# SyncE's transfers limited to five under way, a warm-up of two long matmuls, and inputs of 48 rows in an FFT convolution with two gated MLPs

## The chip, the cores and the metric

The kernel runs on one core of a Trainium2 chip. The metric is the device time of one execution in microseconds; the time before is 1123.38 us, the median of three runs (1122.09 to 1124.87). A profile of one execution comes with it. TensorE, VectorE, ScalarE and GpSimd compute, and SyncE issues the transfers on one queue in program order; 16 DMA engines carry them, and the engines' own code too.

## The reference, cut to what matters

```python
X = np.fft.rfft(x, axis=1)                      # x: (2, 3008, 256)
y = np.fft.irfft(X * (filt_r + 1j * filt_i), n=3008, axis=1)
x = y.reshape(6016, 256)
g = x @ w_gate                                  # first MLP, d_ff 1536
x = (g / (1 + exp(-g)) * (x @ w_val)) @ w_out
h = x @ w_in                                    # second MLP, d_ff 2048
out = (h * clip(h + 3, 0, 6) / 6) @ w_out2
```

## The kernel before, in words

The 3008-point transform is split into 47 x 64 points. Its inputs lie in DRAM as 128 rows: rows 0 to 46 hold one half of a column group, rows 64 to 110 the other half, and the rows between are zeros. The matmuls of L332 read only rows 0 to 47 and 64 to 111 (`rows(r, N1P)`, `N1P = 48`).

The transform works in 16 steps of one column group each (`STEPS`, loop `for k in range(N + 2)` at L463). A step k runs `over_n1(k)` (L332: 32 small matmuls, each two passes of 48 columns), then `back(k - 2)` (L374: 8 matmuls of two passes), then a list of transfers (`moves[k]`), then `over_n2(k)` (L348: 8 matmuls of two passes) and `filter_product(k)` (VectorE L361, GpSimd L115 and L118). ScalarE copies between the stages (L339, L340, L379). The list of a step holds `load_x(k + 3)` (steps 1 to 12), two transfers of a filter (`load_filter`, steps 2 to 5), the weights of the first MLP in three parts (`load_dec`, steps 1, 8, 11), and stores of finished quarters to the DRAM tile `d2` (`store`, two in each of the steps 5 to 12, eight in step 13). At step 12 the first halves of two token blocks are loaded back from `d2` (`load_half`, L441), 48 rows at a time, and at step 15 the second halves, which need the eight stores of step 13.

`load_x(k)` fills one of four places in a ring: it waits until `over_n1(k - 4)` has read the place. The first input goes on ScalarE's queue, every other on SyncE's, each in two transfers: by column quarters for k < 2, by column halves of all 128 rows after that. How many transfers are under way is not set by the kernel; the tile framework gives each one of a small set of semaphores in turn.

Ahead of the first input TensorE runs `idle(8)` (L317), eight matmuls of 128 columns on zeros, with a memset before them (L311).

After the transform come the first MLP on the first block (L233, L241), in which the other stores of `d2` and the weights of the first MLP still move, and then both MLPs on all blocks (L680, L725), untouched by the change except that the writes of decoded weights (`low_w1`, L404) and `load_dec` now go through the new helper.

Of the kernel before, what the change touches and what calls it, by code (L numbers as in the profile page):

```python
# [16 lines left out]
P = 128  # L17
B, S, D = 2, 3008, 256
N1, N2 = 47, 64
N1P = 48  # L20
# [57 lines left out]
def fft_conv_glu_mlp(ctx: ExitStack, tc: tile.TileContext, x, filt, mats, sgn, w1, w2, out):  # L78
    nc = tc.nc
    w1, w2 = w1.bitcast(U32), w2.bitcast(U32)  # L80
# [9 lines left out]
    sg = keep.tile([P, NK], F32, name="sg")  # L90
# [7 lines left out]
    def wall(f):  # L98
        return wall_a[:, f] if f < 8 else wall_b[:, f - 8]


    d2 = [dram.tile([NK, P, D], F32, name=f"d2_{b}") for b in range(B)]
    yd = [dram.tile([P, 4, 512], F32, name=f"yd_{k}") for k in range(len(BLOCKS))]
    w1f = [dram.tile([P, 10 * P], F32, name=f"w1f_{f}") for f in range(F1)]
# [5 lines left out]
    def bank(tag="gv"):  # L110
        turn[tag] += 1
        return banks[tag][(turn[tag] - 1) % 4]

    def minus(out, a, b, engine=None):
        (engine or nc.vector).tensor_tensor(out=out, in0=a, in1=b, op=ALU.subtract)  # L115
# [9 lines left out]
    def rows(i, n=64):  # L125

        return slice(i * 64, i * 64 + n)
# [4 lines left out]
    def turns(first, n):  # L132

        return 32 * first // N1, -(-(32 * first + n // 2) // N1)
# [132 lines left out]
    with tc.manual_schedule():  # L267
# [7 lines left out]
        fl = [a[:, :3072].rearrange("p (j r n) -> p j r n", j=4, r=2) for a in (x0, side)]  # L275
        ring = work.tile([P, 7168], F32, tag="xs", name="ring")
        turned = work.tile([P, 7168], F32, tag="xs", name="turned")[:, :6144].rearrange("p (b q c) -> p b q c", b=2, c=P)
        room = new_y()

        N, RING = 16, 2  # L280
        STEPS = [(b, 4 * a + i) for a in range(2) for b in range(B) for i in range(4)]
        xin, first, spec, acc2 = {}, {}, {}, {}

        def load_x(k, engine=nc.sync):
            b, j = STEPS[k]
            if k % 2 == 0:
                xin[k // 2] = ring[:, k // 2 % RING * 2048:(k // 2 % RING + 1) * 2048].rearrange("p (a n) -> p a n", a=2)
            to, src = (v.rearrange("p (o i n) -> p i o n", o=2, i=2) if k < 2 else v.rearrange("p (i n) -> p i n", i=2)
                       for v in (xin[k // 2][:, k % 2], x[b, j // 2, :, j % 2]))
            for i in range(2):  # L290
                engine.dma_start(out=to[:, i], in_=src[:, i])

        def load_filter(j):
            for r in range(2):
                nc.sync.dma_start(out=fl[j // 4][:, j % 4, r], in_=filt[j][:, r])

        load_x(0, nc.scalar)
        load_x(1)
        nc.sync.dma_start(out=sg, in_=sgn)
        load_filter(0)  # L300
        load_filter(1)
        load_x(2)
        load_filter(2)
        load_x(3)
        load_filter(3)
# [1 line left out]
        nc.gpsimd.memset(warm, 0.0)  # L307
        nc.scalar.activation(out=warm, in_=warm, func=AF.Silu)

        blank = turned[:, 1, 0]  # L310
        nc.vector.memset(blank, 0.0)  # L311

        def idle(n):

            acc = bank()
            for _ in range(n):
                nc.tensor.matmul(acc[:, :P], blank, blank)  # L317

        idle(8)

        def prepare_filter(j):

# [57 lines left out]

        def store(b, a, i):
            q = slice(i * NK // 8, (i + 1) * NK // 8)
            nc.sync.dma_start(out=d2[b][q, :, a * P:(a + 1) * P].rearrange("q p c -> p q c"), in_=turned[:, b, q])  # L383

        def words(a):
            return a.bitcast(U32).rearrange("p (n t) -> p n t", t=2)
# [3 lines left out]
        def load_dec(f, n=1):  # L390
            a = x0[:, (f + 1) % 2 * 3072:]
            dec[f] = Decode(None, None, 768, (words(a[:, :1536]), a[:, 1536:2304], a[:, 2304:3072]))
            raw = dec[f].raw.rearrange("p n t -> p (n t)")
            for i in range(n):
                c = slice(1536 * i // n, 1536 * (i + 1) // n)
                nc.sync.dma_start(out=raw[:, c], in_=w1[:, f, c])

        def high_w1(f):
            nc.scalar.copy(out=wall(f)[:, 0], in_=dec[f].w)
# [1 line left out]
        def low_w1(f, engine=None):  # L401
            w = dec.pop(f).w
            minus(wall(f)[:, 1], w, wall(f)[:, 0].bitcast(F32), engine)
            nc.sync.dma_start(out=w1f[f][:, :6 * P], in_=w)  # L404

        todo = {}

# [9 lines left out]
        for k, f in ((1, 0), (8, 1), (11, 2)):  # L417
            send(k, load_dec, f, 3)
        for j in range(4, 8):
            send(j - 2, load_filter, j)  # L420
        for i in range(8):
            send((5, 5, 6, 6, 7, 7, 8, 8)[i], store, 0, 0, i)
            send((9, 9, 10, 10, 11, 11, 12, 12)[i], store, 1, 0, i)
            send(13, store, 0, 1, i)

        for f, steps in ((0, (4, 5, 5, 6, 7, 8, 9, 10, 10)), (1, (10, 11, 11, 12, 12, 13, 14, 15, 17)), (2, (15, 15, 15, 17))):
            at(steps[0], lambda f: dec[f].start(), f)
            for i in range(len(steps[1:7])):
                at(steps[1 + i], lambda f, i: dec[f].part(i, nc.vector), f, i)
            if f < 2:  # L430
                at(steps[7], high_w1, f)
                at(steps[8], low_w1, f)
            else:
                for i in range(3, 6):
                    at(N + 1, lambda f, i: dec[f].part(i, nc.vector), f, i)

        def load_half(j, a, g):
            t0, t1 = turns(FIRST[j][0], 512)
            g = g[:, :7 * P].rearrange("p (t c) -> p t c", c=P)
            for r in range(2):  # L440
                nc.sync.dma_start(out=g[rows(r, N1P), :t1 - t0],  # L441
                                  in_=d2[0].rearrange("q (h n) c -> (q h) n c", h=2)[:, 32 * r + t0:32 * r + t1, a * P:(a + 1) * P])
            return g

        half_accs = {}
# [17 lines left out]
        for k in range(N + 2):  # L463
            if 1 < k < N:
                over_n1(k)
            if 2 <= k <= N:
                back(k - 2)
            for step, *a in moves.get(k, ()):
                step(*a)
            if k == 12:  # L470
                g0 = new_g()
                gt[0] = [load_half(0, 0, g0)]
                gt[1] = [load_half(1, 0, room[:, 6 * COLS:])]
            elif k == N - 1:
                gt[0].append(load_half(0, 1, g0[:, 7 * P:]))
                gt[1].append(load_half(1, 1, turned[:, 0].rearrange("p q c -> p (q c)")))
            if k < N:
                over_n2(k)
                filter_product(k)
            elif k == N:  # L480
                for j in range(2):
                    form(j, 0)
                    form_end(j, 0)
            if k < 3 or 3 < k < 8:
                prepare_filter(k + (k < 3))
            for step in todo.get(k, ()) if k <= N else ():
                step()
# [80 lines left out]
        for t in range(2 * plain):  # L568
            p, i = divmod(t, 2)
            k, g_ = steps[p]  # L570
            f = 2 * g_ + i
# [8 lines left out]
            if t == 0:  # L580
                pairs = []
                for u in range(2):
                    if u:
                        back(N - 1)
                        turn["gv"] -= 2
                        for step in todo[N + 1][:3]:
                            step()
                        load_dec(3)
                        form(0, 1)
                        form_end(0, 1)  # L590
                        for step in todo[N + 1][3:]:
                            step()
                    pairs.append((bank(), bank()))
                    gate, val = pairs[u]
                    for part in ((0, 1, 2),) if u else ((0, 2), (1,)):
                        l1(gate, wall(u), (3 * P, 4 * P), xsd[k], part, depth=(0,))
                        l1(val, wall(u), (0, 5 * P), xsd[k], part, depth=(0,))
# [13 lines left out]
            h = hid[p][:, i]  # L611
            nc.scalar.activation(out=h, in_=gate, func=AF.Silu)

            lead, rest, part = ([f_ for f_ in range(2, F1) if t == 2 * f_ + d + (f_ > 9)] for d in (-6, -5, -4))
# [7 lines left out]
            for f_ in part:  # L622
                low_w1(f_, nc.gpsimd)
                if f_ + 2 < F1:
                    load_dec(f_ + 2)
# [16 lines left out]
            if 10 < t < 23:  # L642
                q, r = divmod(t - 11, 2)
# [86 lines left out]
        class Plain:  # L730
            kind, k, f, n, last = 0, 0, 0, 512, True
# [125 lines left out]
        for s in range(S):  # L857
# [15 lines left out]
            k, f, n, kind = u.k, u.f, u.n, u.kind  # L873
# [121 lines left out]
```

## Time and profile before

| What | Value |
|---|---|
| median of three runs | 1123.38 us |
| the profiled execution | 1120.58 us, span 1118.8 |
| TensorE, matmuls | 1108.6 us, 99% of the span |
| VectorE | 858.3 us, 77% |
| ScalarE | 751.9 us, 67% |
| GpSimd | 602.3 us, 54% |
| chain of waits, TensorE's share | 94% |
| HBM read, written | 117.27 MB, 32.24 MB |

The transform takes about the first 58 to 75 us of the span, two of the page's 40 slices. A row of the chain of waits gives the start, the length and who holds the chain; "issue" is time in which an engine waits for nothing that the profile shows. Rows of SyncE (SPq) give the time that issuing takes, not the transfer. The end of a matmul is modelled, so a group's end is later than the start of what follows it.

### The profile page before, as it was taken

The page shows a single profiled execution, that of the slowest core. Times are in us where ns is not written, and L with a number is a line of the kernel's source. Part 1 is how long each engine was busy: PE and PEld are TensorE (multiplying, and loading weights), DVE is VectorE, ACT ScalarE, POOL GpSimd, SP SyncE. Part 2 cuts the span into 40 slices and gives each one's busy share as a digit, 9 for nine tenths or more (in the row PEclk, how much of TensorE's full clock was granted, in tenths as well). Part 3 has the DMA queues.
Part 4 walks back from the last instruction along what each step waited for, and adds up shares of the span by engine and source line. Part 5 has one row for each costly group of instructions (what it writes and reads, how often), then busy time and mean ns, then how long its engine had stood idle before and what let it go on. Part 6 is the DMA issues. An engine that isn't in the chain of part 4 may idle for free.

```text
span 1118.8 us, 19197 instructions
## 1 busy us (share of the span) xinstructions
PE 1108.6 (99%) x7246; PEld 924.9 (83%) x7246; DVE 858.3 (77%) x1168; ACT 751.9 (67%) x1367; POOL 602.3 (54%) x779
## 2 busy tenths in 40 slices
PE   9999999999999999999999999999999999999998
PEld 7678887888888888888899888888888888888997
DVE  5889976778878788786888868667677677677765
ACT  4554447667767667766777777777777677677764
POOL 4652375795765576484587645335435444354440
PEclk9999999999999999999999999999999999999999
DMA  9974954844633552263353421422322412412300
GB/s 315 296 210 132 278 186 157 223 152 134 200 118 111 147 176 100 83 202 104 102 208 120 162 82 60 153 78 71 135 78 78 144 62 78 149 52 77 117 27 33
DMA packets 58844, 150.75 MB, mean 135 GB/s; under 512 B 5568, under 2 KB 26016, under 8 KB 56992
## 3 DMA queue, kind: packets, MB, share of 16 engines
q1 hardware_dynamic: 58208, 149.01, 41.4%
q8 instruction: 56, 0.92, 0.3%
q10 hardware_dynamic: 544, 0.52, 0.2%
q14 instruction: 36, 0.29, 0.1%
HBM read 117.27 MB, written 32.24 MB: 134 GB/s over the span
## 4 chain that ended last, share of the span: by engine, by line
PE 94%; DVE 3%; DMA 1%; ACT 1%; issue 1%; SPq 0%; ACTq 0%; DVEq 0%
PE gv L680 44%; PE a L725 36%; PE gv L233 5%; PE a L241 2%; PE gv L374 2%; PE a L348 1%; PE gv L332 1%; PE gv L157 1%; DVE hs L115 1%; DVE h L707 1%; DVE xs L115 1%; DMA ring<-x_in 0%; DVE raw L115 0%; SPq L383 0%; DMA d<-turned 0%
## 5 line engine op out<-in xcount | busy, mean ns | idle before, releaser
L680 PE MATMUL gv<-xs,wu 128*128 128x512 f32 (+1 forms) x2268 | 567.1, 386 | 0.1
L115 POOL TENSOR_TENSOR wu<-st,wu 128x224 fp32r<-128x224 f32 x432 | 311.9, 753 | 397.0 <-ACT wu L517 397.0
L680 PEld LDWEIGHTS gv<-xs,wu 128*128 128x128 f32 x2268 | 423.7, 188 | 81.3 <-ACT raw L546 1.7
L725 PE MATMUL a<-hs,wo 128*128 128x512 f32 (+1 forms) x1872 | 476.7, 385 | 0.0
L725 PEld LDWEIGHTS a<-hs,wo 128*128 128x128 f32 x1872 | 351.4, 188 | 65.4 <-ACT hs L713 0.3
L115 DVE TENSOR_TENSOR hs<-h,hs 128x512 fp32r<-128x512 f32 (+3 forms) x228 | 235.4, 1033 | 66.8 <-ACT hs L713 62.3
L713 ACT CAST hs<-h 128x512 fp32r<-128x512 f32 (+3 forms) x216 | 172.6, 799 | 128.8 <-DVE h L709 73.9
L115 POOL TENSOR_TENSOR wo<-st,wo 128x256 fp32r<-128x256 f32 x156 | 148.8, 967 | 0.0
L709 DVE SCALAR_TENSOR_TENSOR h<-h,gv 128x512 f32<-128x512 f32 (+1 forms) x144 | 96.5, 670 | 22.7 <-ACT h L703 22.4
L517 ACT CAST wu<-st 128x384 fp32r<-128x384 f32 x216 | 110.6, 563 | 0.3 <-DMA st<-w1f 0.3
L701 ACT ACTIVATE h<-gv 128x512 f32<-128x512 f32 (+1 forms) x120 | 70.7, 589 | 58.3 <-PE gv L680 57.2
L118 DVE TENSOR_TENSOR gv<-gv,h 128x512 f32<-128x512 f32 (+1 forms) x108 | 74.0, 685 | 41.4 <-PE gv L680 35.7
L703 ACT ACTIVATE h<-gv 128x512 f32<-128x512 f32 (+1 forms) x144 | 84.1, 584 | 15.3 <-PE gv L680 15.1
L890 ACT COPY gv<-gv 128x512 f32<-128x512 f32 (+1 forms) x108 | 60.9, 564 | 42.6 <-PE gv L680 38.4
L118 DVE TENSOR_TENSOR h<-gv,h 128x512 f32<-128x512 f32 (+1 forms) x108 | 72.9, 675 | 18.5 <-PE gv L680 18.1
L709 DVE SCALAR_TENSOR_TENSOR h<-h,h 128x512 f32<-128x512 f32 (+1 forms) x48 | 32.7, 681 | 58.6 <-ACT h L703 58.6
L894 ACT COPY h<-gv 128x512 f32<-128x512 f32 (+1 forms) x108 | 62.5, 579 | 16.4 <-PE gv L680 13.4
L707 DVE TENSOR_TENSOR h<-h 128x512 f32<-128x512 f32 (+1 forms) x60 | 61.4, 1023 | 1.7 <-ACT h L701 1.0
L115 DVE TENSOR_TENSOR xs<-raw,xs 128x512 fp32r<-128x512 f32 (+1 forms) x77 | 58.9, 767 | 0.1
L517 ACT CAST wo<-st 128x256 fp32r<-128x256 f32 (+1 forms) x108 | 54.2, 501 | 0.0
L560 ACT CAST xs<-raw 128x512 fp32r<-128x512 f32 (+1 forms) x77 | 45.7, 609 | 2.9 <-DVE raw L115 2.8
L233 PE MATMUL gv<-xs,wall_a 128*128 128x512 f32 x192 | 45.7, 392 | 0.1
(88 smaller groups left out, 899.7 us busy)
## 6 DMA issues: line engine op xcount, KB each, us to landing
st<-w1f SPq DMA_DIRECT2D x60, 576.0 KB, 3.8
st<-w2f SPq DMA_DIRECT2D x48, 704.0 KB, 4.1
raw<-w_in SPq DMA_DIRECT2D x16, 512.0 KB, 4.6
ring<-x_in SPq DMA_DIRECT2D x30, 256.0 KB, 5.5
x<-w_in SPq DMA_DIRECT2D x9, 768.0 KB, 5.4
d<-turned SPq DMA_DIRECT2D x32, 192.0 KB, 5.3
yd<-y SPq DMA_DIRECT2D x5, 1024.0 KB, 6.5
raw<-yd SPq DMA_DIRECT2D x5, 1024.0 KB, 6.3
```

What stands on the lines that cost most here:

```text
L115: (engine or nc.vector).tensor_tensor(out=out, in0=a, in1=b, op=ALU.subtract)
L118: (engine or nc.vector).tensor_tensor(out=out, in0=a, in1=b, op=ALU.add)
L233: nc.tensor.matmul(acc, w[:, r, c[k]:c[k] + P], xs[:, v, k], start=(r, v, k) == (0, 0, 0), stop=(r, k) == (1, 1), skip_group_check=len(dep ...
L517: nc.scalar.copy(out=to[:, 0, at:at + hi - lo], in_=src[:, lo:hi])
L680: nc.tensor.matmul(acc[:, :n], w[:, r, FORM[a] * P:(FORM[a] + 1) * P], xs_part(k, v, i), start=start and q == 0, stop=q == 2, skip_group_c ...
L701: nc.scalar.activation(out=self.value(t, 0), in_=src, func=AF.Silu)
L703: nc.scalar.activation(out=self.value(t, a), in_=src, func=AF.Relu, bias=3.0)
L707: nc.vector.tensor_tensor(out=self.value(t, 0), in0=self.value(t, 0), in1=src, op=ALU.mult)
L709: nc.vector.scalar_tensor_tensor(out=self.value(t, a), in0=self.value(t, a), scalar=6.0, in1=src, op0=ALU.min, op1=ALU.mult)
L713: nc.scalar.copy(out=self.hs[:, t, :, 0, :self.n], in_=self.value(t))
L725: yield lambda t=t, v=v, a=a, j=j, r=r: nc.tensor.matmul(banks["a"][2 * j + t][:, :n], self.wo[:, r, (2 * a + j) * P:(2 * a + j + 1) * P], ...
L894: nc.scalar.copy(out=u.s7, in_=b3[:, :n])
```

## The change

A helper `move` replaces the direct calls in the transform. It keeps a list of SyncE's transfers and makes each one wait for the landing of the fifth before it. Inputs from the third on are read as two transfers of 48 whole rows (4 KB a row) in place of two of 128 half rows (2 KB a row). The memset and the idle matmuls are four times as wide, and there are two in place of eight.

```diff
-        N, RING = 16, 2
+        N, RING, MOST_UNDER_WAY = 16, 2, 5
+        under_way = []
+
+        def move(to, src, engine=nc.sync):
+
+            ins = engine.dma_start(out=to, in_=src)
+            if engine is nc.sync:
+                if len(under_way) >= MOST_UNDER_WAY:
+                    tc.add_manual_dep(ins.ins, under_way[-MOST_UNDER_WAY].ins.name,
+                                      mybir.DependencyInfo(mybir.DependencyClass.Sync, mybir.DependencyReason.DATA),
+                                      reason="few transfers under way")
+                under_way.append(ins)
...
-            to, src = (v.rearrange("p (o i n) -> p i o n", o=2, i=2) if k < 2 else v.rearrange("p (i n) -> p i n", i=2)
-                       for v in (xin[k // 2][:, k % 2], x[b, j // 2, :, j % 2]))
+            to, src = xin[k // 2][:, k % 2], x[b, j // 2, :, j % 2]
+            if k < 2:
+                to, src = (v.rearrange("p (o i n) -> p i o n", o=2, i=2) for v in (to, src))
             for i in range(2):
-                engine.dma_start(out=to[:, i], in_=src[:, i])
+                part = (slice(None), i) if k < 2 else rows(i, N1P)
+                move(to[part], src[part], engine)
...
-        blank = turned[:, 1, 0]
+        blank = turned[:, 1, 0:4].rearrange("p q c -> p (q c)")
         nc.vector.memset(blank, 0.0)
...
-                nc.tensor.matmul(acc[:, :P], blank, blank)
-
-        idle(8)
+                nc.tensor.matmul(acc, blank[:, :P], blank)
+
+        idle(2)
```

The filters, the sign table, the stores, `load_dec`, the writes of `low_w1` and `load_half` call `move` in the same way; `load_g`, `load_wq` and what follows the transform do not.

## Rows read from the trace of the kernel before

**Rows 1.** Chain of waits, 11 to 56 us: start, length (us), what held it.
```profile
11.54 0.86 issue
...
21.98 1.17 PE a L348 x15
...
25.63 1.17 PE a L348 x15
...
27.67 0.25 issue
...
33.25 0.31 issue
...
43.54 1.06 issue
...
49.95 1.39 issue
...
55.72 1.17 PE a L348 x14
```

**Rows 2.** The page, parts 1 and 3: records of TensorE, packets of its code.
```profile
PE 1108.6 (99%) x7246; PEld 924.9 (83%) x7246; DVE 858.3 (77%) x1168; ACT 751.9 (67%) x1367; POOL 602.3 (54%) x779
...
q8 instruction: 56, 0.92, 0.3%
```

**Rows 3.** Transfers from 42.20 to 43.25 us: all packets, and those of code.
```profile
DMA packets 40, 0.07 MB, mean 69 GB/s; under 512 B 5, under 2 KB 18, under 8 KB 38
...
q8 instruction: 1, 0.02, 5.8%
```

**Rows 4.** Busy us of each engine by stretch, clock, DMA share, GB/s.
```profile
10.00:20.00 10.00, 9.14 (x238) 6.94 (x232) 7.74 (x16) 4.29 (x12) 7.67 (x12) 1.00 1.00 349
...
30.00:40.00 10.00, 9.69 (x270) 7.51 (x266) 9.73 (x16) 4.87 (x14) 7.37 (x10) 1.00 1.03 328
...
58.00:60.00 2.00, 2.00 (x32) 1.40 (x26) 2.00 (x4) 1.85 (x6) 1.56 (x3) 1.00 1.03 268
70.50:72.00 1.50, 1.38 (x87) 1.27 (x79) 1.47 (x3) 1.50 (x5) 1.50 (x3) 1.00 1.16 179
117.50:119.50 2.00, 2.00 (x10) 1.66 (x9) 1.97 (x3) 1.09 (x3) 0.00 (x0) 1.00 1.01 135
```

**Rows 5.** SyncE's issues, 12 to 18 us; from the page, KB and us to landing.
```profile
12.43 1.52 SPq L396 DMA_DIRECT2D x<-w_in  x3
...
17.17 0.85 SPq L291 DMA_DIRECT2D ring<-x_in  x2
...
ring<-x_in SPq DMA_DIRECT2D x30, 256.0 KB, 5.5
```

**Rows 6.** Instructions in order of time, 0 to 13 us: start, us.
```profile
0.83 0.17 DVE L311 MEMSET turned<- 128x128 f32 x1 [0.83 <-PEq L980]
...
4.76 1.11 PE L332 MATMUL gv<-mat,ring 48*64 48x48 f32 x32
...
6.17 1.61 PE L332 MATMUL gv<-mat,ring 48*64 48x48 f32 x96 [0.30 <-DMA ring<-x_in]
...
11.80 0.91 POOL L115 TENSOR_TENSOR h<-h 128x192 f32<-128x192 f32 x1
...
12.76 1.74 PE L374 MATMUL gv<-h,mat 64*64 64x384 f32 x14
```

**Rows 7.** SyncE and TensorE in order of time, 52 to 75 us.
```profile
52.87 0.98 SPq L291 DMA_DIRECT2D ring<-x_in  x2
...
60.29 5.43 SPq L383 DMA_DIRECT2D d<-turned  x8
...
64.19 1.21 PE L332 MATMUL gv<-mat,ring 48*64 48x48 f32 x60
...
68.36 0.82 SPq L441 DMA_DIRECT2D g<-d  x2
...
74.84 0.84 PE L157 MATMUL a<-mat,g 48*64 48x47 f32 x48
```

More of the change, by code (lines that the diff above doesn't have):

```diff
@@ L287, in load_x @@
                 xin[k // 2] = ring[:, k // 2 % RING * 2048:(k // 2 % RING + 1) * 2048].rearrange("p (a n) -> p a n", a=2)
-            to, src = (v.rearrange("p (o i n) -> p i o n", o=2, i=2) if k < 2 else v.rearrange("p (i n) -> p i n", i=2)
-                       for v in (xin[k // 2][:, k % 2], x[b, j // 2, :, j % 2]))
+            to, src = xin[k // 2][:, k % 2], x[b, j // 2, :, j % 2]
+            if k < 2:
+                to, src = (v.rearrange("p (o i n) -> p i o n", o=2, i=2) for v in (to, src))
             for i in range(2):
-                engine.dma_start(out=to[:, i], in_=src[:, i])
+                part = (slice(None), i) if k < 2 else rows(i, N1P)
+                move(to[part], src[part], engine)
         def load_filter(j):
             for r in range(2):
-                nc.sync.dma_start(out=fl[j // 4][:, j % 4, r], in_=filt[j][:, r])
+                move(fl[j // 4][:, j % 4, r], filt[j][:, r])
         load_x(0, nc.scalar)
         load_x(1)
-        nc.sync.dma_start(out=sg, in_=sgn)
+        move(sg, sgn)
         load_filter(0)
@@ L382, in store @@
             q = slice(i * NK // 8, (i + 1) * NK // 8)
-            nc.sync.dma_start(out=d2[b][q, :, a * P:(a + 1) * P].rearrange("q p c -> p q c"), in_=turned[:, b, q])
+            move(d2[b][q, :, a * P:(a + 1) * P].rearrange("q p c -> p q c"), turned[:, b, q])
         def words(a):
@@ L395, in load_dec @@
                 c = slice(1536 * i // n, 1536 * (i + 1) // n)
-                nc.sync.dma_start(out=raw[:, c], in_=w1[:, f, c])
+                move(raw[:, c], w1[:, f, c])
         def high_w1(f):
@@ L403, in low_w1 @@
             minus(wall(f)[:, 1], w, wall(f)[:, 0].bitcast(F32), engine)
-            nc.sync.dma_start(out=w1f[f][:, :6 * P], in_=w)
+            move(w1f[f][:, :6 * P], w)
         todo = {}
@@ L440, in load_half @@
             for r in range(2):
-                nc.sync.dma_start(out=g[rows(r, N1P), :t1 - t0],
-                                  in_=d2[0].rearrange("q (h n) c -> (q h) n c", h=2)[:, 32 * r + t0:32 * r + t1, a * P:(a + 1) * P])
+                move(g[rows(r, N1P), :t1 - t0], d2[0].rearrange("q (h n) c -> (q h) n c", h=2)[:, 32 * r + t0:32 * r + t1, a * P:(a + 1) * P])
             return g
```

## The prediction

> **What bounds the kernel now.** I read the page first: TensorE is busy for 99% of the span and nearly all of the chain of waits is TensorE, so only time in which it stands still can be won. I then took the chain of waits in order of time over the transform, since the change touches nothing later. It is a loop of three kinds of TensorE work per step (L332, L374, L348), and the reader should see two things in it. The L348 pieces of undisturbed steps start 3.65 us apart (21.98, 25.63), and five times the chain stands at "issue", a wait for nothing that the profile shows: 0.86, 0.25, 0.31, 1.06 and 1.39 us, together 3.87 us [rows 1].
>
> These look like waits for TensorE's own code. They stand in the middle of an L332 or an L374 group whose operands are all there. The page counts 7246 + 7246 records on TensorE and 56 packets (0.92 MB, so 16 KB each) in its instruction queue, one per 259 records [rows 2]; a step has 64 + 16 + 16 passes, 192 records, so a block lasts 1.35 steps. For the 1.06 us stop I cut the transfers to a window: the block arrives between 42.20 and 43.25 us, when hardly anything else moves (69 GB/s) [rows 3]; TensorE goes on at 44.61. So the block came late. Why is seen around it: from 10 to 20 and from 30 to 40 us the 16 DMA engines are at a share of 1.00 and 1.03 [rows 4], and SyncE issues far ahead. In four rows, of which the first and the last are shown, it issues nine transfers from 12.43 to 18.02 us, and one takes some 5.5 us to land [rows 5]: about eight are under way, and the block stands among them.
>
> **The change, part by part.** The sum is made against the profiled execution, 1120.58 us (span 1118.8 and 1.8 around it). The median of the runs shown is 1123.38, 2.8 us more; I add the difference to that.
>
> *Stops for code.* From the L348 piece at 21.98 to that at 55.72 lie eight steps [rows 1]: 33.74 us where 8 x 3.65 = 29.20 would do, an excess of 4.54. Four of the stops lie in between (3.01 us); the other 1.5 us is what a stop costs beyond what is shown, because the last passes before it are drawn until they drain and the loop needs a step to settle. With five under way instead of eight, a block that waits as a transfer does would come after 5/8 of 5.5 us, some 3.4 us, and blocks are wanted some 4.9 us apart (1.35 x 3.65). I take all 4.54 us back here; the bounds are 0 and 4.54. Something is lost to VectorE: from 30 to 40 us it is busy for 9.73 of 10 us [rows 4], so a loop that is 12% faster there (4.54 of 38 us) can't all be had in those steps; later ones have room. 0.3 us, from 0 to 0.5.
>
> The first stop (0.86 us at 11.54) gives nothing: the L374 passes behind it start at 12.76, and GpSimd hands over their operand at 11.80 + 0.91 = 12.71 [rows 1, 6].
>
> *Warm-up.* Two matmuls of 512 columns instead of eight of 128: the same 1024 columns. Its memset takes 0.17 us for 128 columns; for 512 it is between 0.17 and 0.68, so the warm-up starts and ends 0 to 0.5 us later [rows 6]. [...] I take 0.
>
> *The cap at the start.* load_x(0) is on ScalarE's queue and does not count. The first wait is that of filter 1, for load_x(1). From there each SyncE instruction waits for the landing five back, and all issues behind it wait with it. The third input is wanted at about 10.2 us, and even at 11.6 it would be in time for the L374 at 12.76, whose operand comes from GpSimd. I take 0, from 0 to +0.5.
>
> *Inputs as 48 rows.* Bytes fall from 2 x 256 KB to 2 x 192 KB per input. What a byte costs is the disputed term. 128-row loads move at 349 GB/s with the engines full (10 to 20 us) [rows 4]. The loads of 48 rows that the kernel already has (g) do not: with the engines as full, 135 GB/s in the long ones and 179 in the short ones at 70.5 us, where nothing was queued ahead; but 268 in 58 to 60 us, where the short ones stood in a deep queue among stores [rows 4]. So a pair that costs 524 KB / 349 = 1.50 us now costs 393 KB / 268 = 1.47 us at best and 393 KB / 135 = 2.9 us at worst. A queue of five is between the two: I take 200 GB/s, 1.97 us, +0.47 us per input. [...]
>
> [...]
>
> *Is that hidden?* The last input is issued at 52.87 and 53.4, lands 5 to 5.5 us later at about 58.7, and is used at 64.19: 5.5 us of slack [rows 5, 7]. If TensorE comes 4.5 us earlier, 1.0 is left. The inputs 5 to 15 are read while the engines are full: 11 x 0.47 = 5.2 us later. So 5.2 - 1.0 = 4.2 us of waiting for inputs takes the place of the stops, at 200 GB/s. Not all of these steps are full (42.2 to 43.25 us is nearly empty), and stores and filters between them keep their price; I take off 0.7 for that one gap: 3.5.
>
> *The end of the transform.* The eight stores at 60.29 are let go by ScalarE, and behind them wait the four loads of the second half (from 68.36 on), first read by L157 at 74.84 [rows 7]. At the 179 GB/s of that window two of 147 KB need 1.65 us; with the 2 us or so that pass before it, some 2 to 3 us of slack stand before 74.84. With five under way the last stores come up to 0.5 us later, which this slack covers while TensorE is only about 1 us ahead; if it were 4 ahead, the stores would be let go earlier too.
>
> Sum: -4.54 + 3.5 = -1.04 us, and with VectorE's 0.3 -0.7; between the two I take -1.0. 1120.58 - 1.0 = 1119.6, and on the median 1122.4.
>
> **Rivals.** *Faster: the halves run side by side.* For it: 268 GB/s at 58 to 60 us in a queue, and the bytes fall by a quarter. Then an input costs 1.47 us, the slack of 1.0 is enough, and all stops go: -4.54 + 0.3 (VectorE) = -4.2, 1119.2 on the median. [...]
>
> *Slower: inputs become the bound.* For it: 135 to 179 GB/s wherever 48-row loads stood alone. At 165 GB/s, between these two, a pair costs 2.38 us, +0.88; 11 x 0.88 - 1.0 = 8.7 us of starving against 4.54 won: +4.2, 1127.6. It decides where the pair costs more than 1.50 + (4.54 + 1.0)/11 = 2.0 us, below 196 GB/s. The last slack of the stores goes with it.
>
> *No change: the cap does not bring the code earlier.* If a block waits for a fixed share of work whatever is queued, the stops stay, inputs stay hidden behind them and the time is 1123.4, within 0.5. For it: at 42.2 us the block came late though little else moved. [...]
>
> **How the numbers follow.** Chances: forecast 0.37, side by side 0.30, inputs the bound 0.18, no change 0.15. The forecast's own range is 1119.5 to 1125 (150 to 230 GB/s in part of the steps). The range over all, with the 1.3 us by which runs differ, is 1118.3 to 1127.3. A measurement tells 0.3%, 3.4 us, from no change: faster means under 1120.0, slower over 1126.8. Side by side lands under 1120.0 in four of five cases (0.24) and the forecast in one of six (0.06): 0.30. Slower: 0.12 of the 0.18 and 0.03 of the forecast: 0.15. Between: 0.55.
>
> **What would show it.** In the chain after: no "issue" pieces over 0.2 us in the L332 and L374 groups (if they stay, the third rival). "DMA ring<-x_in" as what ends L332's idle time, some 3.5 us in all; none if the halves run side by side, over 7 if inputs are the bound. GB/s at a full share between 15 and 50 us: near 200 in the forecast, 270 or more in the first rival. The L348 piece of step 12 starts at 55.72 now [rows 1]; I expect 54 to 55. I am wrong in the main if TensorE waits neither for code nor for inputs and the time still stands, or if something after 75 us moves.

## The result and the profile after

The changed kernel takes 1127.21 us (median of 11 runs, 1125.12 to 1132.41), the kernel before 1121.06 us on the same chip (11 runs): a ratio of 1.0057, 95% interval 1.0042 to 1.0073, 6 us slower. I had forecast 1122.4, 1 us below the 1123.38 known then, too little to tell from no change. The profiled execution took 1126.81 us (span 1125.0); its clock is 1.00 throughout. The lines of the kernel moved: L332 is L346, L348 is L362, L374 is L388, L379 is L393, and every transfer of the transform is issued in L285.

The chain of waits of the changed kernel, the pieces that answer to [rows 1] and the whole end of the transform (start, length, what held it):

```profile
12.65 1.08 PE gv L346 x59
...
20.00 4.63 DMA ring<-x_in
...
29.35 0.38 issue
...
48.78 2.53 DMA ring<-x_in
...
58.49 1.17 PE a L362 x15
...
62.09 3.42 DMA ring<-x_in
...
65.54 4.67 DMA g<-d
...
70.23 3.61 DMA d<-turned
...
73.85 2.76 DMA d<-turned
...
77.06 3.38 DMA g<-d
...
80.48 0.89 PE a L157 x40
```

The stops for code are gone: of 3.87 us of "issue" pieces one of 0.38 is left. In their place stand transfers. The piece at 48.78 is named after the input that was issued then, but that input landed at 52.15. What let ScalarE go on at 51.31 was the last of the early stores of `turned`, issued at 46.77 and landed at 51.21, and TensorE waited for ScalarE (the idle time stands in brackets):

```profile
51.31 0.86 ACT L393 COPY turned<-gv 128x384 f32<-128x384 f32 x2 [4.61 <-DMA ring<-x_in]
51.94 1.80 PE L388 MATMUL gv<-h,mat 64*64 64x384 f32 x16 [2.98 <-ACT turned L393]
```

ScalarE may not overwrite `turned` before its store has landed.

From 62.09 on the chain is nothing but transfers of 2.8 to 4.7 us, each released by the landing of one before it. Up to the store at 73.85 that is the cap, drawn as a chain; the loads behind it need the stores, as they did before. The L348 piece of step 12 (now L362) starts at 58.49 in place of 55.72, and L157's second half at 80.48 in place of 74.84 [rows 7], 5.64 us later. Nothing behind it gives this back or adds much: 1126.81 - 1120.58 is 6.2.

The start, the windows, and SyncE, as in [rows 4 to 7]; then SyncE's longest waits up to 85 us (total, times, longest):

```profile
0.91 0.48 DVE L325 MEMSET turned<- 128x512 f32 x1 [0.91 <-PEq L993]
5.17 2.56 PE L346 MATMUL gv<-mat,ring 48*64 48x48 f32 x128
12.26 0.95 PE L346 MATMUL gv<-mat,ring 48*64 48x48 f32 x25 [1.48 <-DMA ring<-x_in]
```

```profile
10.00:20.00 10.00, 8.43 (x203) 6.38 (x200) 7.31 (x15) 4.22 (x12) 7.30 (x12) 1.00 0.89 221
30.00:40.00 10.00, 10.00 (x230) 7.67 (x224) 9.84 (x17) 6.42 (x18) 7.83 (x11) 1.00 0.86 230
```

```profile
15.85 3.12 SPq L285 DMA_DIRECT2D x<-w_in  x3
...
62.09 1.52 SPq L285 DMA_DIRECT2D ring<-x_in  x2
...
68.51 5.77 SPq L285 DMA_DIRECT2D d<-turned  x8
76.69 0.91 SPq L285 DMA_DIRECT2D g<-d  x2
```

```profile
SPq L285 <- DMA ring<-x_in: 13.5, 22, 1.7
SPq L285 <- DMA d<-turned: 6.1, 10, 1.8
SPq L285 <- DMA x<-filt_in: 4.1, 3, 1.8
```

The engines are no longer full (shares 0.89 and 0.86 where they were 1.00 and 1.03) and yet TensorE waits for data: SyncE stands still until an earlier transfer lands, 24 us in these three rows; before, the longest row of this kind was 3.8 us (inputs). The first load of w_in and the last input are 52 transfers apart in the program, in both kernels. Before, SyncE needed 40.44 us for them (12.43 to 52.87), now 46.24 (15.85 to 62.09). The eight stores of step 13 go out at 68.51 in place of 60.29, the loads of the second half at 76.69 in place of 68.36.

### The profile page after: what moved, and what is told of

Same layout as the page of the kernel before. It is cut to its first block, busy times and chain, and to the rows that moved or that the text cites. A ratio compares the mean times of both kernels' runs of the same rounds, so it can differ in the third digit from the quotient of the medians.

```text
span 1125.0 us, 19173 instructions
## 1 busy us (share of the span) xinstructions
PE 1109.7 (99%) x7234; PEld 921.3 (82%) x7234; DVE 857.2 (76%) x1168; ACT 751.7 (67%) x1367; POOL 603.2 (54%) x779
## 4 chain that ended last, share of the span: by engine, by line
PE 93%; DMA 3%; DVE 3%; ACT 1%; issue 0%; SPq 0%; ACTq 0%; DVEq 0%
PE gv L693 44%; PE a L738 36%; PE gv L233 5%; PE a L241 2%; DMA ring<-x_in 2%; PE gv L157 1%; PE gv L388 1%; PE a L362 1%; PE gv L346 1%; DMA g<-d 1%; DVE hs L115 1%; DVE h L720 1%; DMA d<-turned 1%; DVE xs L115 1%; DVE raw L115 0%
## 5 line engine op out<-in xcount | busy, mean ns | idle before, releaser
L115 POOL TENSOR_TENSOR wo<-st,wo 128x256 fp32r<-128x256 f32 x156 | 151.3, 983 | 0.0
```

## Experiments

I first held that the 48-row transfers were to blame, as in my rival on inputs, and that the cap by itself wins. The rival theory was that five transfers under way cannot carry the load, whatever their rows. The first four kernels take the change apart.

**The cap alone.** The kernel before with `move` and the cap of five in every place, inputs and warm-up as they were:

```diff
-                engine.dma_start(out=to[:, i], in_=src[:, i])
+                move(to[:, i], src[:, i], engine)
```

> The kernel before with the cap of five alone: inputs stay two transfers of 128 half rows, the warm-up stays eight short matmuls. Theory (the 48-row rows cost the time, the cap wins the stops for code): faster than before by 1.5 to 4 us, no 'issue' piece over 0.4 us between 10 and 55 us in the chain, transfers of x near 300 GB/s or more in 20 to 50 us, the form matmuls of L157 start before 74.84. Rival (five under way cannot keep the engines full, whatever the rows): slower than before by 4 to 8 us, TensorE waits for inputs as in the changed kernel and 20 to 50 us moves about 230 GB/s.

Measured: 1129.91 us, ratio 1.0089 (1.0074 to 1.0104). My theory fell: the cap alone costs more than the whole change. In its chain every long piece is again a transfer, and TensorE stops for 3.31 us because ScalarE may overwrite `turned` only when its late stores have landed (at 53.08; ScalarE goes on at 53.18). TensorE's timeline:

```profile
46.67 1.47 PE L386 MATMUL gv<-h,mat 64*64 64x384 f32 x14
...
53.80 2.66 PE L386 MATMUL gv<-h,mat 64*64 64x384 f32 x16 [3.31 <-ACT turned L391]
```

**The 48 rows alone.** The kernel before, with only this:

```diff
...
+            to, src = xin[k // 2][:, k % 2], x[b, j // 2, :, j % 2]
...
+                part = (slice(None), i) if k < 2 else rows(i, N1P)
+                engine.dma_start(out=to[part], in_=src[part])
```

> The kernel before with the 48-row inputs alone: no cap, the old warm-up. [...] Rival (the cap is what starves): eight under way hide the latency, within 1 us of before or faster by up to 2 us since a quarter of the input bytes goes.

Measured: 1120.77 us, ratio 1.0005 (0.9994 to 1.0017): no change, where my theory had it as slow as the changed kernel. The rival held. Its windows and a piece of its chain:

```profile
10.00:20.00 10.00, 8.17 (x194) 5.48 (x192) 7.63 (x15) 3.89 (x11) 7.67 (x12) 1.00 1.07 254
20.00:30.00 10.00, 9.41 (x251) 7.62 (x243) 5.63 (x11) 5.45 (x14) 4.82 (x8) 1.00 1.06 236
```

```profile
18.61 0.60 issue
```

Without a cap the 48 rows do move slowly, 236 to 254 GB/s at a share over 1.0 where 128 rows had 349 [rows 4], and the stops for code stay (2.5 us in all). That a quarter fewer input bytes makes up for it is likely, but not shown by itself.

**Cap and warm-up, 128 half rows.** The changed kernel with the input lines of before:

```diff
-                part = (slice(None), i) if k < 2 else rows(i, N1P)
-                move(to[part], src[part], engine)
+                move(to[:, i], src[:, i], engine)
```

> The changed kernel with its inputs put back to two transfers of 128 half rows: cap and new warm-up stay. Theory (rows): as the cap alone, within 1 us, so faster than before by 1.5 to 4 us; against the changed kernel that is 7 to 10 us won by the rows alone. Rival (the cap): slower than before by 4 to 8 us. Rival (the warm-up costs): slower than the cap alone by over 1 us.

Measured: 1132.91 us, ratio 1.0115 (1.0099 to 1.0131). So under a cap of five the 48 rows win some 6 us (1.0115 against 1.0057), a part of it by the clock (0.65 from 50 to 58 us here, 1.00 in the changed kernel). The 3 us over the cap alone looked like a price of the warm-up; the run of the warm-up alone, below, shows none. The two profiled spans are equal (1130.6), and what else differs between them is the clock after a stop (0.79 in the cap alone from 50 to 58 us); I leave it open.

**The same bytes over all rows.** The changed kernel, but inputs from the fifth on as 128 rows of 384 of the 512 columns; a quarter of the columns is left out.

```diff
...
+                    c = slice(512 * i, 512 * i + (512 if k < 4 else 384))
+                    move(to[:, c], src[:, c], engine)
```

> The changed kernel, cap and warm-up kept, but inputs from the fifth on as two transfers of 128 rows and 384 of 512 columns: the same bytes as the 48-row transfers (2 x 192 KB), over all rows. A quarter of the input columns is left out. Theory (the rows' place, not the bytes): faster than before by 2 to 4.5 us, at least as fast as with whole 128-row halves; an input lands 3 us or less after issue. Rival (fewer bytes or the number of transfers decide, not where they go): as the changed kernel, +6 us.

Measured: 1126.43 us, ratio 1.0059 (1.0040 to 1.0078): the changed kernel's time. Where the rows lie decides nothing here. With that my first theory is dead and the rival is left: a number under way, divided by a time to land. The next runs put it to the test as theory A.

**Seven under way.**

```diff
-        N, RING, MOST_UNDER_WAY = 16, 2, 5
+        N, RING, MOST_UNDER_WAY = 16, 2, 7
```

> The changed kernel with seven transfers under way in place of five. Theory A (the cap sets the pace: so many under way, divided by the 4.3 us that one takes to land, is fewer transfers than the steps want): with seven at 5 us one lands every 0.71 us, and 53 transfers take 38 us in place of 47; within 1.5 us of before, 5 to 7 us faster than the changed kernel. Theory B (waiting for one given earlier transfer, however far back, holds SyncE's queue): still 3 us or more slower than before.

Measured: 1120.09 us, ratio 0.9989 (0.9977 to 1.0001). Theory A held. No stop for code is left in TensorE's work, and the gain is small all the same; its chain says what is late next:

```profile
48.30 0.60 POOL h L115
48.89 0.55 POOL h L118
49.44 1.27 POOL h L115
50.71 0.56 POOL h L118
51.27 0.62 issue
51.89 1.95 DVE h L375 x4
```

From 44 to 60 us VectorE and GpSimd hold the loop, with the filter products and, between them, VectorE's decoding of weights (the 0.62 is behind a GpSimd piece, not in TensorE's work).

**Fewer, larger transfers under five.** Each filter in one transfer, stores two quarters at a time; same bytes.

```diff
-            for r in range(2):
-                move(fl[j // 4][:, j % 4, r], filt[j][:, r])
+            move(fl[j // 4][:, j % 4], filt[j])
...
+            if i % 2:
+                return
+            q = slice(i * NK // 8, (i + 2) * NK // 8)
```

> The changed kernel, five under way, same bytes, but each filter's two transfers and each two stores of neighbouring quarters go as one: 43 transfers in place of 54 between 16 and 63 us. Theory A (the number under way against the time to land): the latest input lands 5 us or more earlier than in the changed kernel (66.1 us), and the time is within 2 us of before. Rival C (the bytes or the 48 rows limit, the number does not matter): as the changed kernel, +6 us.

Measured: 1121.48 us, ratio 1.0004 (0.9992 to 1.0016). Theory A held in the time: five slots suffice when each holds more. The last input lands at 61.6 us, some 4.5 earlier than in the changed kernel, where I had said 5 or more. From its page (transfers, KB each, median us to landing):

```profile
d<-turned SPq DMA_DIRECT2D x16, 384.0 KB, 5.1
ring<-x_in SPq DMA_DIRECT2D x28, 192.0 KB, 4.8
```

**No cap from step 13 on.**

```diff
-                if len(under_way) >= MOST_UNDER_WAY:
+                if len(under_way) >= MOST_UNDER_WAY and not ending:
...
+            if k == 13:
+                ending.append(k)
```

> The changed kernel, but from step 13 on (eight stores, the second halves of the token blocks and what follows) SyncE's transfers do not wait for the fifth before. Theory A in two parts: of the 5.6 us by which the first form matmul (L157) is late, 2.8 come before step 12's over_n2 and as much behind it; if the cap on the stores makes the second part, L157 starts at 77 to 78 us in place of 80.5 and the time is +2.5 to +3.5 us against before. Rival: the second part is only the first passed on and grown by the inputs; then nothing changes, +6 us.

Measured: 1126.16 us, ratio 1.0044 (1.0029 to 1.0058), L157 at 79.52. Mostly a miss: about 1 us of the 2.8 comes back. Its chain:

```profile
61.58 4.25 DMA ring<-x_in
...
65.84 0.78 SPq L285
...
70.90 1.43 SPq L285
...
72.37 3.08 DMA d<-turned
...
75.90 3.57 DMA g<-d
```

The stores no longer wait for landings, but they stand behind the late inputs on SyncE's queue, and nine issues after each other take until 72.33. So the end is late mainly because the inputs were issued late.

**The warm-up alone**, in the kernel before:

```diff
-        idle(8)
+        idle(2)
```

with the wide memset and matmul of the change.

> The kernel before with the short warm-up alone (two matmuls of 512 columns, the wider memset). My forecast: no change, within 1 us. Rival (with the cap the short warm-up came with 3 us more, so it costs by itself): slower than before by 2 to 3 us.

Measured: 1121.73 us, ratio 0.9998 (0.9986 to 1.0009): no change, as forecast. Its chain shows something else by the way. Transfers and inputs are those of before, and the stops in its L332 and L348 work are these two:

```profile
43.44 0.57 issue
...
50.11 0.62 issue
```

1.19 us where the execution that I predicted from had 3.87, and yet its profiled execution is only 0.7 us shorter (1119.85 against 1120.58). How often the code comes late differs, though only the warm-up is another.

**Four and six under way.**

```diff
-        N, RING, MOST_UNDER_WAY = 16, 2, 5
+        N, RING, MOST_UNDER_WAY = 16, 2, 4
```

> The changed kernel with four under way. Theory A, now as a sum: transfers issued per us are the number under way over the time to land. Time to land was 5.10 us with seven, 4.21 with five, so I expect 3.8 with four; 3.8 over 3.75 really under way is 1.0 us for each, 53 transfers take 53.6 us (47.4 with five), the last input lands at about 72 us, and the time is 11 to 13 us over before (6 over the changed kernel). Theory B (the engines are slower on 48 rows and set the pace, not the cap): time to land falls to 3.4 us, the pace stays at 0.9, time as the changed kernel, +6.

Measured: 1137.68 us, ratio 1.0141 (1.0113 to 1.0169), 16.6 us over before: the direction of theory A, the size missed by 4 to 5. The pace came out as expected (0.995 us); what I had not counted, and what I take the rest to be, is the longer stops and a lower clock behind them (0.93, 0.86 and 0.77 in its windows from 50 to 58, 58 to 66 and 85 to 100 us).

> The changed kernel with six under way. Theory A: 4.65 us to land over 5.65 under way is 0.82 us for each, the 53 transfers take 43.6 us, 3.8 us less than with five; the steps want 0.77. The time is between 0 and 2.5 us over before. Theory B: +4 or more.

Measured: 1122.03 us, ratio 1.0009 (0.9996 to 1.0022), as theory A said. The rows of the four pages, from four to seven under way:

```profile
ring<-x_in SPq DMA_DIRECT2D x28, 192.0 KB, 3.7
```

```profile
ring<-x_in SPq DMA_DIRECT2D x28, 192.0 KB, 4.2
```

```profile
ring<-x_in SPq DMA_DIRECT2D x28, 192.0 KB, 4.7
```

```profile
ring<-x_in SPq DMA_DIRECT2D x28, 192.0 KB, 5.3
```

With SyncE's rows (start of the first load of w_in, start of the last input, 52 transfers between) they make one table:

| Under way | us to land | start to start, us | us for each | land / under way | ratio |
|---|---|---|---|---|---|
| 4 | 3.7 | 17.39 to 69.12 | 0.995 | 0.93 | 1.0141 |
| 5 (the change) | 4.2 | 15.85 to 62.09 | 0.889 | 0.84 | 1.0057 |
| 6 | 4.7 | 14.43 to 55.95 | 0.798 | 0.78 | 1.0009 |
| 7 | 5.3 | 14.55 to 54.94 | 0.777 | 0.76 | 0.9989 |
| 48 rows, no cap | 5.8 | 13.75 to 53.08 | 0.756 | | 1.0005 |

Before needs 0.778 us for each. It has 7.0 transfers under way in the mean of this stretch, by their issues and landings, not the eight that I had read; so a cap of seven takes next to nothing away. From four to seven the time to land grows by 0.53 us a transfer, not in proportion: of 3.7 us with four, some 1.6 (3.7 - 4 x 0.53), an estimate from these rows, are there whatever the number. By it a cap pays that part on every slot; what the 1.6 us consist of, no run here shows. At six and seven, land / under way is down to what the steps ask for; at five and four it is above, and the time follows.

**Seven under way, 128 half rows throughout.** The kernel of cap and warm-up with seven:

```diff
-        N, RING, MOST_UNDER_WAY = 16, 2, 5
+        N, RING, MOST_UNDER_WAY = 16, 2, 7
```

> Seven under way and the short warm-up, but all inputs as 128 half rows. Theory A: 230 KB in the mean instead of 200 take longer to land (with five under way 4.63 in place of 4.21), so seven give about 0.85 us for each: 1 to 4 us slower than before. Rival (with seven the engines are full, and 128 rows then move at 349 GB/s where 48 rows had 240 to 260): as fast as 48 rows under seven or faster, -1 to -3 us against before.

Measured: 1120.45 us, ratio 0.9994 (0.9981 to 1.0007). Between the two: one transfer each 0.81 us where theory A said 0.85, and no loss that can be told where it said 1 to 4 us. So a pace a little over 0.778 still costs nothing here.

**Seven, 128 half rows for the first eight inputs, then 48 rows.**

```diff
+                part = (slice(None), i) if k < 2 else (slice(None), slice(512 * i, 512 * i + 512)) if k < 8 else rows(i, N1P)
```

> A version that might beat both: seven under way, 128 half rows up to the eighth input, when the engines are full (share 1.03, 238 to 264 GB/s with 48 rows), and 48 rows behind it. If those early inputs were what is left to win, the fourth and later inputs land 1 to 2 us earlier than with 48 rows throughout, and the time is 2 to 4 us below before. Rival (VectorE and GpSimd hold the chain there now): as with seven and 48 rows throughout, -1 us.

Measured: 1118.42 us, ratio 0.9975 (0.9961 to 0.9988): 2.7 us faster than before, the one kernel that beats both. Early windows, the stops left in its chain, and L157:

```profile
10.00:20.00 10.00, 9.10 (x241) 6.75 (x236) 7.74 (x16) 4.29 (x12) 7.69 (x12) 1.00 0.94 324
20.00:30.00 10.00, 9.72 (x252) 7.50 (x248) 7.40 (x15) 6.55 (x18) 6.54 (x11) 1.00 0.98 297
```

```profile
27.79 0.28 issue
...
43.24 0.41 issue
...
58.56 0.35 issue
```

```profile
72.27 0.84 PE L157 MATMUL a<-mat,g 48*64 48x47 f32 x48
```

324 and 297 GB/s where 48 rows gave 264 and 238 under the same cap, 1.04 us of stops, and L157 at 72.27 in place of 74.84.

**The same inputs without a cap, and under five.** What does each half of that version do? First the kernel before with these inputs:

```diff
+                part = (slice(None), i) if k < 2 else (slice(None), slice(512 * i, 512 * i + 512)) if k < 8 else rows(i, N1P)
+                engine.dma_start(out=to[part], in_=src[part])
```

> The inputs of the version with seven (128 half rows up to the eighth input, 48 rows behind it) in the kernel before: no cap, old warm-up. If the cap of seven wins its 2.7 us by bringing TensorE's code earlier, this one still has stops for code of 1.5 to 3 us in all and is within 1 us of before. Rival (the mixture of inputs wins it, the cap adds nothing): 2 to 3 us faster than before, the stops gone or paid for by it.

Measured: 1119.81 us, ratio 0.9994 (0.9983 to 1.0005), within 1 us of before, with one stop in its TensorE work and a late last part of w_in:

```profile
29.16 0.91 issue
...
51.06 5.13 DMA x<-w_in
```

The time is as my theory said, the reason is not shown: the stops are 0.91 us here and 1.04 with seven. That the cap of seven adds something is likely by the ratios, whose intervals just overlap; that it does so through the code is not shown.

Then the changed kernel, five under way, with the same line for `part`:

> The changed kernel with five under way and the same mixture of inputs. Theory A (under way over time to land): 4.4 us to land over 4.75 is 0.93 us for each, as slow as the changed kernel or a little slower, +6 to +9 us. Rival (the early 48-row inputs under full engines are what the change loses): most of it is back, within 2 us of before.

Measured: 1126.62 us, ratio 1.0058 (1.0041 to 1.0075). Theory A held in the time, with one transfer each 0.845 us in place of the 0.93 that it gave: faster rows early do not help when five slots set the pace.

## Why the prediction was wrong

**The failing step: the cap had no price after the start.** Under "Stops for code" I wrote that five under way in place of eight would bring things in after "5/8 of 5.5 us, some 3.4 us". That takes it that the time to land shrinks with the number under way, so that the engines stay full and no transfer is lost. It shrank to 4.2. The cost follows from the rows that I had: before, one transfer goes out each 0.778 us; five slots allow 3.9 us to land; with 4.2 over the 4.8 that are under way in the mean, it is one each 0.889, and 52 x 0.11 = 5.8 us more for the same list. I priced the cap at the start (0 to 0.5 us) and for the last stores (0.5 us, hidden); the steps between had no price.

**Stops for code, -4.54.** The direction was right, the size was not. That the stops are waits for code is borne out: in the sixteen profiled executions there are 30 of them over 0.15 us between 8 and 75 us, and each ends 1.2 to 1.7 us after a block of code has landed, while blocks land some 5 us apart (before: blocks at 11.00, 26.34, 31.97, 43.20 and 49.97, TensorE going on at 12.40, 27.92, 33.56, 44.61 and 51.34). Two things made the term too large. The sum of the stops differs: 3.9 us in the execution that I read, 2.5 (48 rows), 1.2 (warm-up) and 0.9 (mixed inputs) in the three others without a cap, 2.1 in the mean; in the twelve with a cap it is between 0 and 1.6, 0.6 in the mean. So a cap seems to take some 1.5 us of stops away, a third of what I took back, and the two ranges overlap. And with the stops gone the loop does not run at 3.65 us a step. Under seven no stop is left, and the eight steps of [rows 1] still take 31.3 us (start of the first to start of the last):

```profile
22.42 1.75 PE L362 MATMUL a<-y,mat 64*64 64x384 f32 x16
...
53.70 1.75 PE L362 MATMUL a<-y,mat 64*64 64x384 f32 x16
```

Against 33.74 that is some 2.5 us, not 4.54; VectorE and GpSimd hold the chain next, and I had put that at 0.3. In the time of a whole execution the stops hardly show: the four without a cap, in the order above, took 1120.58, 1120.29, 1119.85 and 1120.64 us (single executions, two of them with other inputs). Seven with mixed inputs is 2.7 us faster than before; that this comes from the stops is not shown.

**48 rows, +3.5 us.** Wrong in sign under the cap. 48 rows without a cap: 1.0005. With five: 1.0057 against 1.0115 for 128 half rows. The rate I took (200 GB/s) was a price for full engines, and they are not full under five; there, fewer bytes land sooner (4.2 us against 4.5 for 128 half rows under five, 0.889 us for each against 0.946). Without a cap 48 rows moved at 236 GB/s at a share of 1.06 (20 to 30 us), but that does not set the time: there it was that of before, and under five the same bytes over all rows gave 1.0059.

**The rival "inputs become the bound"** gave 1127.6, nearly the time measured, by luck: it was +4.2 us on a median of 1123.38, measured was +6.2 on 1121.06. (My range over all ended at 1127.3, so it left this rival's own time out.) Its reason was wrong too: inputs are the bound because they are issued late, not because a pair costs 2.38 us. Its test, "DMA ring<-x_in" as what ends L332's idle time with over 7 us in all, was not met either: L346 waits 2.0 us for inputs in front of its matmuls, and the rest of the loss shows elsewhere: at 51.31, in the wait for the store of `turned` (2.98 us of TensorE); and at the end of the transform. My sign of GB/s at a full share could not be read: from 15 to 50 us the share is 0.92, at 236 GB/s.

**The start.** The third input came late: L346 at 12.26 in place of about 10.2, outside what I had allowed. As argued, little of it lasts: the next step's passes begin 0.7 us later.

**The end.** My slack of 2 to 3 us was right. Before, the two loads of `g` land 3.0 and 3.5 us after their issue, the second at 72.2, some 2.7 us ahead of L157. In the changed kernel the loads of the second half go out 8.33 us later (76.69 against 68.36) and L157 starts 5.64 later, so 2.7 us were covered. What I had not seen is that the cap would push the whole list on SyncE back by 9.2 us (62.09 against 52.87).

**The warm-up, 0.** Right, in the run of it alone (ratio 0.9998); the wide memset takes 0.48 us, inside my 0.17 to 0.68. **No change, the cap does not bring code earlier:** the time moved, and that by another way; the stops did get fewer.

## What to carry to other kernels

Before a limit on transfers under way is set, divide: the list's length and the time that it has give the us for each, and the number under way times that is the time to land that can be afforded. The time to land didn't fall in proportion to the number here (5.3 us with seven, 3.7 with four), so take it from runs at several limits rather than by scaling; if it doesn't fit, raise the limit or put more bytes in each transfer. A stop in one profiled execution is not yet a price: look whether another execution has it too, and how long the steps take where it is gone.

## What the runs showed of the hardware

After stops of TensorE of 2 to 3.5 us inside the transform its granted clock was lower in some executions, and the length of the stop alone does not tell in which. In the kernel with the cap alone the granted clock from 50 to 58 us is 0.79, and the sixteen L386 passes behind the stop of 3.31 us take 2.66 us, where fourteen took 1.47 above. With the same bytes over all rows a stop of 2.15 us was followed by the same 0.79; with one of 2.98 us the changed kernel's profiled execution kept 1.00. So a late transfer was paid for a second time in some of them, and this differs from run to run: the mean clock of the changed kernel's eleven runs lies between 0.994 (the slowest, 1132.41 us) and 1.000.

TensorE goes on 1.2 to 1.7 us after the block of code that it waited for has landed, in all 30 stops.
